# Eight PSUM banks in one rotation, and both halves of an expert's first layer open at once

## The chip, the core and the metric

One Trainium2 chip, one of its cores. The metric is the device time of one execution in microseconds, the median of several runs. The engines are TensorE (PE in the profile, with PEld for its weight loads), VectorE (DVE), ScalarE (ACT), GpSimd (POOL) and SyncE (SP), which issues most of the transfers.

## The reference

An mLSTM cell over 4 batches, 8 heads, 768 steps and 40 channels gives 3072 rows of 320 numbers. Each row then goes through one of 8 experts, chosen by a hash of its token, which is a two-layer network with 1024 hidden units:

```python
def _moe_ref(x, token_ids, w1, w2):          # x (3072, 320), w1 (8, 320, 1024), w2 (8, 1024, 320)
    expert_idx = token_ids * np.int64(2654435761) % np.int64(E)
    out = np.zeros((N, D), dtype=np.float32)
    for e in range(E):
        mask = expert_idx == e
        if not mask.any():
            continue
        xe = x[mask]
        h = np.maximum(xe @ w1[e], 0.0)
        out[mask] = h @ w2[e]
    return out.astype(np.float32)
```

Everything is fp32.

## The kernel before

The first 140 us or so compute the mLSTM cell in chunks of 128 steps, sort the tokens by expert and store the rows of the result in memory. The change does not touch that part. Its PSUM pool is closed before the experts begin.

**Experts.** The rows of an expert lie in 416 slots (CAP): three tiles of 128 and a remainder of 32. Expert 0 is computed plainly, half of its first layer already inside the mLSTM part. Experts 1 to 7 pass through the loop `for e in range(E)`, whose order of calls is the order in which each engine receives its instructions; no scheduler moves them (`tc.manual_schedule()`). For an expert e from 1 on that order is:

1. `fetch(e + 2)`: POOL gathers the rows of a later expert, SP stores them to memory and reads them back in blocks (`blocks`); `load_weights(e + 2)` on SP.
2. `differences_of_w2`: four POOL operations for the second layer (tile `tw`).
3. `layer1_by_seven`: the first layer.
4. POOL copies the remainder columns of h into `hrem`.
5. `layer2` for the third tile of 128 slots: eight matmuls of 320 columns (L1030), then ACT copies the result out and POOL scatters it.
6. `sums_of_w1` for the next expert, four DVE operations (tile `sw`).
7. After experts 3 and 7, `rest`: the second layer of four experts' remainders (L1143).
8. `layer2_by_seven`: the second layer for the other two tiles of slots, 4 x 7 matmuls of 160 columns (L1063). In its middle (`meanwhile`) DVE makes the differences of the next expert's rows (`sums_of_x`, tile `tx`).

**The first layer.** Of the 320 inputs the first 256 are two blocks of 128 rows, and the last 64 are a half block. The two full blocks, two blocks of hidden units and two halves of the slots make a 2 x 2 x 2 product, which is computed with seven block products in place of eight, in Winograd's form: sums of w1's blocks (`sw`) are multiplied with differences of the rows (`tx`). DVE and ACT put the products together with the intermediate tiles m, u and v. The 64 inputs are added by `halves` (L996): matmuls that use 64 of the array's 128 rows, issued in pairs, one on the lower and one on the upper rows, into two different banks.

The layer is done in two halves, g = 0 and g = 2, each with four blocks of hidden units. A half uses four PSUM banks and issues, on PE: products 0, 1, 2, 3 and 0 again (10 matmuls, L988), eight matmuls of 64 rows (L996), products 2 and 3 again (4 matmuls, L988). `product` issues two matmuls each time. After the first five products of the half g = 0 comes `meanwhile(g)`, which for experts 3 to 6 is a DVE transpose of the next expert's rows (`turned`, L1129). At the end of each half `done(g)` makes the sums of h for the second layer (`sums_of_h`, L942 to L945, tile `sh`): on POOL for g = 0, on DVE for g = 2.

**PSUM.** The pool `mps` has three kinds of tiles: `tp` for transposes and `zp` for second-layer results, two buffers each, and `mh` with four. Each of the first layer's halves takes all four `mh`, and so does `layer2_by_seven`. The second half of a layer therefore takes the banks of the first half.

**Buffers.** m1, u2 and u4 have one buffer each, `tx` has two. h (tile `h0`) is the same tile for all experts.

Of the kernel before, what the change touches and what calls it, by code (L numbers as in the profile page):

```python
# [8 lines left out]
F32 = mybir.dt.float32  # L9
# [8 lines left out]
P = 128  # L18
# [4 lines left out]
def kernel(  # L23
# [24 lines left out]
    nc = tc.nc  # L48
# [4 lines left out]
    Dm = H * D  # L53
    E, _, F = moe_w1.shape
    FB = F // P
# [8 lines left out]
    DB = len(dch)  # L64
# [49 lines left out]
    W = {}  # L114
# [790 lines left out]
    xp = ctx.enter_context(tc.tile_pool(name="xp", bufs=2))  # L905
    mps = ctx.enter_context(tc.tile_pool(name="mps", bufs=2, space=PSUM))

    def scatter(zp, idx, apart):
        zo = xp.tile([P, Dm], F32, name="zo", bufs=4)
        nc.scalar.copy(zo[:], zp[:])  # L910
        scatter_rows(zo, idx, apart)

    def scatter_rows(zo, idx, apart):
# [8 lines left out]

    def turn(xg, dst, on_act):

        tp = mps.tile([P, DB, P], F32, name="tp")
        for db in range(2):
            nc.tensor.transpose(tp[:, db, :], xg[:, db * P : (db + 1) * P], ident[:])
        nc.vector.tensor_copy(xg[:, Dm:], xg[:, 2 * P : Dm])
        nc.tensor.transpose(tp[:, 2, :], xg[:, 2 * P :], ident[:])
        if on_act:  # L930
            nc.scalar.copy(dst, tp[:])
        else:
            nc.vector.tensor_copy(dst, tp[:])

    def bank(i):
        return mps.tile([P, CAP], F32, name="mh", bufs=4)

    HC, HD = CAP // 2, Dm // 2

# [20 lines left out]

    def sums_of_x(xT):

        tx = xp.tile([P, 4, HC], F32, name="tx")
        b = [xT[:, i, j * HC : (j + 1) * HC] for i in range(2) for j in range(2)]
        differences(*b, [tx[:, i] for i in range(4)], nc.vector)
        return tx

    def layer1_by_seven(w, sw, xT, tx, h, meanwhile, done):

        w1t, w1c, _ = w  # L970
        lo, hi = slice(0, HC), slice(HC, CAP)

        def add(o, a, b):
            nc.vector.tensor_tensor(o, a, b, op=ALU.add)  # L974

        def pair(t):
            return t.rearrange("p (a c) -> p a c", a=2)

        for g in range(0, FB // 2, 2):
            bank = [mps.tile([P, CAP], F32, name="mh", bufs=4) for _ in range(4)]  # L980
            hv = h[:, 2 * g : 2 * g + 4].rearrange("p (a i) c -> p a i c", i=2)

            def block(fp, i, j):
                return w1t[:, j, (2 * fp + i) * P : (2 * fp + i + 1) * P]

            def product(n, lhsT, rhs, first=False):
                for a in range(2):
                    nc.tensor.matmul(  # L988
                        pair(bank[n])[:, a], lhsT=lhsT(g + a), rhs=rhs, start=first and a == 0, stop=True, skip_group_check=True,
                    )  # L990

            def halves(first, second):
                for a in range(2):
                    for i, (n, r) in enumerate((first, second)):
                        k = slice(i * P // 2, (i + 1) * P // 2)
                        nc.tensor.matmul(  # L996
                            pair(bank[n])[:, a], lhsT=w1c[k, g + a, :], rhs=xT[k, 2, r], start=False, stop=True, skip_group_check=True,
                        )

            m, u, v = [xp.tile([P, CAP], F32, name=n, bufs=1) for n in ("m1", "u2", "u4")]  # L1000
            product(0, lambda fp: block(fp, 0, 0), xT[:, 0, lo], True)
            nc.scalar.copy(m[:], bank[0][:])
            product(1, lambda fp: sw[:, 1, fp], tx[:, 1], True)
            add(u[:], m[:], bank[1][:])
            product(2, lambda fp: sw[:, 0, fp], tx[:, 0], True)
            add(v[:], m[:], bank[2][:])
            product(3, lambda fp: sw[:, 2, fp], tx[:, 2], True)
            add(v[:], v[:], bank[3][:])
            meanwhile(g)
            product(0, lambda fp: block(fp, 0, 1), xT[:, 1, lo])  # L1010
            halves((0, lo), (1, hi))
            nc.scalar.activation(hv[:, :, 0, lo], pair(bank[0]), AF.Relu)  # L1012
            add(hv[:, :, 1, hi], pair(v), pair(bank[1]))
            nc.scalar.activation(hv[:, :, 1, hi], hv[:, :, 1, hi], AF.Relu)
            halves((2, hi), (3, lo))
            product(2, lambda fp: sw[:, 3, fp], xT[:, 1, hi])
            add(hv[:, :, 0, hi], pair(u), pair(bank[2]))
            nc.scalar.activation(hv[:, :, 0, hi], hv[:, :, 0, hi], AF.Relu)
            product(3, lambda fp: block(fp, 1, 1), tx[:, 3])
            for a in range(2):  # L1020
                o = h[:, 2 * (g + a) + 1, lo]
                add(o, pair(u)[:, a], pair(bank[3])[:, a])
                nc.scalar.activation(o, o, AF.Relu)
            done(g)

    def layer2(w, h, js, idx, apart, between=lambda j: None, within=lambda j, fb: None):
        for j in js:
            zp = mps.tile([P, Dm], F32, name="zp")
            for fb in range(FB):
                nc.tensor.matmul(  # L1030
                    zp[:], lhsT=h[:, fb, j * P : (j + 1) * P], rhs=w[2][:, fb, :],
                    start=(fb == 0), stop=(fb == FB - 1),
                )
                within(j, fb)
            scatter(zp, idx(j), apart)
            between(j)
# [15 lines left out]
    def layer2_by_seven(w, tw, h, sh, idx, meanwhile):  # L1052

        w2t = w[2]
        bank = [mps.tile([P, CAP], F32, name="mh", bufs=4)[:, :HD] for _ in range(4)]
        m, u, v = [xp.tile([P, CAP], F32, name=n, bufs=1)[:, :HD] for n in ("m1", "u2", "u4")]
        zs = [xp.tile([P, Dm], F32, name="zo", bufs=4) for _ in range(2)]
        lo, hi = slice(0, HD), slice(HD, Dm)

        def products(*them):  # L1060
            for f in range(FB // 2):
                for n, lhsT, rhs, first in them:
                    nc.tensor.matmul(  # L1063
                        bank[n], lhsT=lhsT(f), rhs=rhs(f), start=first and f == 0, stop=f == FB // 2 - 1, skip_group_check=True,
                    )

        def rows(i, j):
            return lambda f: h[:, 2 * f + j, i * P : (i + 1) * P]

        def cols(j, r):  # L1070
            return lambda f: w2t[:, 2 * f + j, r]

        def of(t, i):
            return lambda f: t[:, i, f]

        def add(o, a, b):
            nc.vector.tensor_tensor(o, a, b, op=ALU.add)

        products((0, rows(0, 0), cols(0, lo), True), (1, of(sh, 1), of(tw, 1), True))
        nc.scalar.copy(m, bank[0])  # L1080
        add(u, m, bank[1])
        products((2, of(sh, 0), of(tw, 0), True), (3, of(sh, 2), of(tw, 2), True))
        add(v, u, bank[2])
        add(zs[1][:, hi], v, bank[3])
        meanwhile()
        products((0, rows(0, 1), cols(1, lo), False))
        nc.scalar.copy(zs[0][:, lo], bank[0])
        products((2, of(sh, 3), cols(1, hi), False), (3, rows(1, 1), of(tw, 3), False))
        add(zs[0][:, hi], u, bank[2])
        add(zs[1][:, lo], u, bank[3])  # L1090
        for j in range(2):
            scatter_rows(zs[j], idx(j), True)
# [4 lines left out]
    with tc.manual_schedule():  # L1097
# [39 lines left out]
            nc.gpsimd.tensor_copy(xT0[:, :, NM:], remT[:, :, :RM])  # L1137

        def rest(g):
            zp = mps.tile([P, Dm], F32, name="zp")  # L1140
            for fb in range(FB):
                for i in range(EG):
                    nc.tensor.matmul(  # L1143
                        zp[i * RM : (i + 1) * RM, :], lhsT=hrem[g][:, i, fb, :], rhs=W[g * EG + i][2][:, fb, :],
                        start=(fb == 0), stop=(fb == FB - 1),
                    )
            scatter(zp, cols_of(s_idx, NR + g)(0), True)
# [6 lines left out]
        for e in range(E):  # L1154
# [7 lines left out]
            if e == 0:  # L1162
                layer2(W[0], h, range(2), cols_of(s_idx, 0), True, lambda j: j == 0 and turn_third(), lambda j, fb: (j, fb) == (1, FB - 3) and turn_rest())
                layer1(W[0], xT0, h, 2 * P, CAP, bank)
                turned(1)
                tx = sums_of_x(xTs[1])
            else:
                tw = differences_of_w2(W[e])
                sh = xp.tile([P, 4, FB // 2, P], F32, name="sh", bufs=1)
                layer1_by_seven(  # L1170
                    W[e], sw, xTs[e], tx, h, lambda g: g == 0 and 2 < e < E - 1 and turned(e + 1),
                    lambda g: sums_of_h(h, sh, g, nc.vector if g else nc.gpsimd),
                )
            nc.gpsimd.tensor_copy(hrem[g][:, i], h[:, :, NM:])
# [65 lines left out]
```

## Time and profile before

| | us |
|---|---|
| median of three runs | 359.0 |
| the three runs | 355.92, 359.00, 360.87 |
| profiled execution, its own time | 359.64 |
| its span, first to last instruction | 357.6 |
| PE busy in the span | 339.2 (95%) |
| DVE busy | 226.9 (63%) |
| POOL busy | 214.3 (60%) |
| ACT busy | 138.5 (39%) |
| mean granted PE clock | 0.987 |

In the chain of work that ended last, PE has 76% of the span. By line the largest shares are L988 (first layer, 128 rows) with 20%, L1063 (second layer by seven) with 13%, L1030 with 8% and L996 (first layer, 64 rows) with 6%. The starts of experts 1 to 7 on PE are at 160.98, 187.47, 212.84, 242.85, 268.22, 293.59 and 318.96 us; PE's last matmuls end shortly before 349 us, and the rest of the span is the last scatter and the end of the program.

How to read the views: a row of the timeline has start, length, engine, line, operation, output and inputs, shape and count, and in brackets the idle time before it with what ended it. fp32 matmuls and their weight loads are shown as two records per instruction, so eight matmuls of L996 stand as x16. "issue" as a releaser means that nothing the profile shows was waited for.

### The profile page before, as it was taken

The numbers are of one execution on the slowest core, as the hardware profiler recorded it, in microseconds if no ns is written. First come the engines' busy times: TensorE is split into PE (matmuls) and PEld (weight loads), VectorE is DVE, ScalarE is ACT, GpSimd is POOL, SyncE is SP. The second block draws the span as 40 slices with busy tenths as digits, with TensorE's granted clock in tenths as the row PEclk, the third lists the DMA queues.
The fourth block names the chain that finished last, engine by engine and source line by source line (L and its number), as shares of the span: only waits on it lengthen the run. The fifth ranks groups of instructions, "written<-read, shape, count | busy, mean of one in ns | idle before, by whom it ended". The sixth has DMA issues, their size and how long they took to land.

```text
span 357.6 us, 9206 instructions
## 1 busy us (share of the span) xinstructions
PE 339.2 (95%) x3573; PEld 292.5 (82%) x3573; DVE 226.9 (63%) x512; ACT 138.5 (39%) x325; POOL 214.3 (60%) x301
## 2 busy tenths in 40 slices
PE   7899999999999699999999999999999999999990
PEld 6677898888888577788899899689899899898870
DVE  8867897998887551056665777726666757645310
ACT  6676688776675451113213212212313212213200
POOL 8822778899885546407717938816927829329221
PEclk9999999999999899999999999999999999999996
DMA  6699999989989964689878959495486592010010
GB/s 128 115 175 163 178 177 182 198 184 193 190 159 238 245 192 112 172 226 288 220 220 220 303 97 358 119 233 194 114 223 213 114 289 75 0 37 19 17 39 3
DMA packets 162358, 59.18 MB, mean 165 GB/s; under 512 B 140171, under 2 KB 158119, under 8 KB 162313
## 3 DMA queue, kind: packets, MB, share of 16 engines
q1 hardware_dynamic: 158377, 49.05, 58.8%
q0 software_dynamic: 2832, 9.34, 8.1%
q8 instruction: 29, 0.48, 0.6%
q10 hardware_dynamic: 1104, 0.18, 0.3%
q14 instruction: 16, 0.13, 0.1%
HBM read 46.48 MB, written 12.38 MB: 165 GB/s over the span
## 4 chain that ended last, share of the span: by engine, by line
PE 76%; DMA 6%; issue 5%; DVE 4%; SPq 4%; POOL 2%; ACT 1%; ACTq 0%; POOLq 0%; DVEq 0%
PE mh L988 20%; PE mh L1063 13%; PE zp L1030 8%; PE mh L996 6%; PE sp L447 6%; PE tr L390 5%; PE xh L505 5%; PE xh L499 3%; PE ab L405 3%; PE xh L478 2%; SPq L1125 2%; DMA w1t<-in_moe_w_dram 2%; SPq L237 1%; DMA R<-gate_rows 1%; PE zp L1143 1%
## 5 line engine op out<-in xcount | busy, mean ns | idle before, releaser
L914 POOL DMA_INDIRECT out_dram<-zo,s_idx x26 | 27.6, 1061 | 76.5 <-issue 46.7
L1030 PE MATMUL zp<-w2t,h 128*128 128x320 f32 x160 | 45.0, 433 | 0.5 <-ACT h L166 0.5
L974 DVE TENSOR_TENSOR h<-u,mh 128x416 f32<-128x416 f32 (+1 forms) x56 | 25.4, 475 | 25.0 <-PE mh L988 12.7
L1030 PEld LDWEIGHTS zp<-w2t,h 128*128 128x128 f32 x160 | 30.0, 190 | 11.8 <-ACT h L166 0.9
L505 PE MATMUL xh<-v,w 128*64 128x41 f32 x768 | 35.3, 224 | 0.0
L414 ACT ACTIVATE w<-ab 128x512 f32<-128x512 f32 x48 | 26.2, 596 | 19.0 <-PE ab L405 18.1
L453 DVE TENSOR_TENSOR w<-sp,w 128x512 f32<-128x512 f32 x48 | 30.8, 681 | 3.6 <-ACT w L414 3.6
L988 PE MATMUL mh<-tx,sw 128*128 128x208 f32 x168 | 31.9, 340 | 0.7 <-DVE sw L944 0.7
L505 PEld LDWEIGHTS xh<-v,w 128*64 128x64 f32 x768 | 31.5, 140 | 0.0
L988 PEld LDWEIGHTS mh<-tx,sw 128*128 128x128 f32 x168 | 29.7, 190 | 1.0 <-DVE sw L944 1.0
L110 POOL DMA_INDIRECT xg<-x_rows,g_idx x24 | 23.4, 975 | 9.0 <-issue 6.7
L447 PE MATMUL sp<-qT,kT 64*128 64x128 f32 x384 | 28.1, 285 | 0.3 <-ACT qT L395 0.3
L499 PE MATMUL xh<-C,qs 128*64 128x82 f32 x320 | 28.0, 253 | 0.0
L1063 PE MATMUL mh<-tw,sh 128*128 128x160 f32 x168 | 27.4, 299 | 0.0
L522 POOL TENSOR_TENSOR x<-x,og 128x320 f32<-128x320 f32 x24 | 20.6, 864 | 10.7 <-ACT og L439 8.6
L447 PEld LDWEIGHTS sp<-qT,kT 64*128 64x128 f32 x384 | 23.5, 187 | 4.2 <-issue 2.5
L974 DVE TENSOR_TENSOR u<-m,mh 128x416 f32<-128x416 f32 x28 | 16.5, 588 | 13.3 <-PE mh L988 6.8
L1012 ACT ACTIVATE h<-mh 128x416 f32<-128x416 f32 x14 | 7.2, 518 | 44.5 <-PE mh L996 44.5
L1063 PEld LDWEIGHTS mh<-tw,sh 128*128 128x128 f32 x168 | 24.3, 190 | 0.0
L988 PE MATMUL mh<-xT,w1t 128*128 128x208 f32 x112 | 24.3, 339 | 0.0
L996 PE MATMUL mh<-xT,w1c 64*128 64x208 f32 x224 | 23.5, 349 | 0.0
L488 POOL TENSOR_TENSOR C<-C,add 64x164 f32<-64x164 f32 x32 | 16.3, 510 | 9.8 <-ACT add L482 8.6
(241 smaller groups left out, 761.2 us busy)
## 6 DMA issues: line engine op xcount, KB each, us to landing
w2t<-in_moe_w_dram SPq DMA_DIRECT2D x7, 1280.0 KB
w1t<-in_moe_w_dram SPq DMA_DIRECT2D x7, 1024.0 KB
xb<-x_slots SPq DMA_DIRECT2D x84, 52.0 KB
k<-in_k_dram SPq DMA_DIRECT2D x24, 160.0 KB
v<-in_v_dram SPq DMA_DIRECT2D x24, 160.0 KB
og<-in_o_gate_dram SPq DMA_DIRECT2D x24, 160.0 KB
q<-in_q_dram SPq DMA_DIRECT2D x23, 160.0 KB
x_slots<-xg SPq DMA_DIRECT2D x7, 480.0 KB
```

Of the source, the lines that this page charges most:

```text
L110: nc.gpsimd.indirect_dma_start(out=xg, out_offset=None, in_=x_d[:rows, :], in_offset=bass.IndirectOffsetOnAxis(ap=idx, axis=0),)
L414: nc.scalar.activation(w[:, hf], ab[:], AF.Exp)
L447: nc.tensor.matmul(sp[hf][:, j, :], lhsT=d["kT"][r, j, :], rhs=d["qT"][r, j, :], start=True, stop=True)
L453: nc.vector.tensor_tensor(d["w"][:, hf], d["sp"][hf][:], d["w"][:, hf], op=ALU.mult)
L499: nc.tensor.matmul(xh[t, 2 * j : 2 * j + 2, :], lhsT=d["qs"][:, j, t], rhs=Cs[b][c % 2][:, j].rearrange("p h d -> p (h d)"), start=True, s ...
L505: nc.tensor.matmul(hs[t, 2 * j + hf, :], lhsT=d["w"][:, hf, j, t], rhs=d["v"][:, 2 * j + hf, :], start=(c == 0), stop=True, skip_group_che ...
L914: ins = nc.gpsimd.indirect_dma_start(out=out[:, :], out_offset=bass.IndirectOffsetOnAxis(ap=idx, axis=0), in_=zo[:], in_offset=None, bound ...
L974: nc.vector.tensor_tensor(o, a, b, op=ALU.add)
L988: nc.tensor.matmul(pair(bank[n])[:, a], lhsT=lhsT(g + a), rhs=rhs, start=first and a == 0, stop=True, skip_group_check=True,)
L996: nc.tensor.matmul(pair(bank[n])[:, a], lhsT=w1c[k, g + a, :], rhs=xT[k, 2, r], start=False, stop=True, skip_group_check=True,)
L1030: nc.tensor.matmul(zp[:], lhsT=h[:, fb, j * P : (j + 1) * P], rhs=w[2][:, fb, :], start=(fb == 0), stop=(fb == FB - 1),)
L1063: nc.tensor.matmul(bank[n], lhsT=lhsT(f), rhs=rhs(f), start=first and f == 0, stop=f == FB // 2 - 1, skip_group_check=True,)
```

## The change

All tiles of the experts come from one kind of PSUM tile, a full bank of 512 fp32, with eight buffers in one rotation (`psum`). `tp`, `zp` and `mh` become views of it.

`layer1_by_seven` becomes a generator per half, `half_layer`, with three stages, and the two halves advance stage by stage: first stage (ten matmuls) of g = 0, then of g = 2; `meanwhile` after both; second stage (the eight matmuls of 64 rows) of g = 0, then of g = 2; third stage (four matmuls and `done`) of g = 0, then of g = 2. Eight banks are open at once. u2 and u4 become one tile for each half (u20, u22, u40, u42), m1 stays one tile for both, and `tx` has one buffer in place of two. Within the second stage the four pairs of 64 rows of a half are issued together, ahead of the additions.

```diff
+    def psum():
+        return mps.tile([P, 4 * P], F32, name="mh", bufs=8)
...
-        tp = mps.tile([P, DB, P], F32, name="tp")
+        tp = psum().rearrange("p (d c) -> p d c", c=P)[:, :DB]
...
     def bank(i):
-        return mps.tile([P, CAP], F32, name="mh", bufs=4)
+        return psum()[:, :CAP]
...
-        tx = xp.tile([P, 4, HC], F32, name="tx")
+        tx = xp.tile([P, 4, HC], F32, name="tx", bufs=1)
...
-        for g in range(0, FB // 2, 2):
-            bank = [mps.tile([P, CAP], F32, name="mh", bufs=4) for _ in range(4)]
+        def half_layer(g):
+            bank = [psum()[:, :CAP] for _ in range(4)]
...
-            m, u, v = [xp.tile([P, CAP], F32, name=n, bufs=1) for n in ("m1", "u2", "u4")]
+            m, u, v = [xp.tile([P, CAP], F32, name=n, bufs=1) for n in ("m1", f"u2{g}", f"u4{g}")]
             product(0, lambda fp: block(fp, 0, 0), xT[:, 0, lo], True)
...
-            add(v[:], v[:], bank[3][:])
-            meanwhile(g)
+            add(v[:], v[:], bank[3])
             product(0, lambda fp: block(fp, 0, 1), xT[:, 1, lo])
+            yield
             halves((0, lo), (1, hi))
+            halves((2, hi), (3, lo))
             nc.scalar.activation(hv[:, :, 0, lo], pair(bank[0]), AF.Relu)
             add(hv[:, :, 1, hi], pair(v), pair(bank[1]))
             nc.scalar.activation(hv[:, :, 1, hi], hv[:, :, 1, hi], AF.Relu)
-            halves((2, hi), (3, lo))
+            yield
             product(2, lambda fp: sw[:, 3, fp], xT[:, 1, hi])
...
             done(g)
+            yield
+
+        parts = [half_layer(g) for g in range(0, FB // 2, 2)]
+        for stage in range(3):
+            for part in parts:
+                next(part)
+            if stage == 0:
+                meanwhile()
...
     def layer2(w, h, js, idx, apart, between=lambda j: None, within=lambda j, fb: None):
         for j in js:
-            zp = mps.tile([P, Dm], F32, name="zp")
+            zp = psum()[:, :Dm]
...
     def layer2_by_seven(w, tw, h, sh, idx, meanwhile):
...
-        bank = [mps.tile([P, CAP], F32, name="mh", bufs=4)[:, :HD] for _ in range(4)]
-        m, u, v = [xp.tile([P, CAP], F32, name=n, bufs=1)[:, :HD] for n in ("m1", "u2", "u4")]
+        bank = [psum()[:, :HD] for _ in range(4)]
+        m, u, v = [xp.tile([P, CAP], F32, name=n, bufs=1)[:, :HD] for n in ("m1", "u20", "u40")]
...
         def rest(g):
-            zp = mps.tile([P, Dm], F32, name="zp")
+            zp = psum()[:, :Dm]
...
                 layer1_by_seven(
-                    W[e], sw, xTs[e], tx, h, lambda g: g == 0 and 2 < e < E - 1 and turned(e + 1),
+                    W[e], sw, xTs[e], tx, h, lambda: 2 < e < E - 1 and turned(e + 1),
                     lambda g: sums_of_h(h, sh, g, nc.vector if g else nc.gpsimd),
                 )
```

More of the change, by code (lines that the diff above doesn't have):

```diff
@@ L906 @@
     mps = ctx.enter_context(tc.tile_pool(name="mps", bufs=2, space=PSUM))
+    def psum():
+        return mps.tile([P, 4 * P], F32, name="mh", bufs=8)
     def scatter(zp, idx, apart):
         zo = xp.tile([P, Dm], F32, name="zo", bufs=4)
-        nc.scalar.copy(zo[:], zp[:])
+        nc.scalar.copy(zo[:], zp)
         scatter_rows(zo, idx, apart)
@@ L977, in pair, with block @@
             return t.rearrange("p (a c) -> p a c", a=2)
-        for g in range(0, FB // 2, 2):
-            bank = [mps.tile([P, CAP], F32, name="mh", bufs=4) for _ in range(4)]
+        def block(fp, i, j):
+            return w1t[:, j, (2 * fp + i) * P : (2 * fp + i + 1) * P]
+        def half_layer(g):
+            bank = [psum()[:, :CAP] for _ in range(4)]
             hv = h[:, 2 * g : 2 * g + 4].rearrange("p (a i) c -> p a i c", i=2)
-            def block(fp, i, j):
-                return w1t[:, j, (2 * fp + i) * P : (2 * fp + i + 1) * P]
             def product(n, lhsT, rhs, first=False):
@@ L998, in halves @@
                         )
-            m, u, v = [xp.tile([P, CAP], F32, name=n, bufs=1) for n in ("m1", "u2", "u4")]
+            m, u, v = [xp.tile([P, CAP], F32, name=n, bufs=1) for n in ("m1", f"u2{g}", f"u4{g}")]
             product(0, lambda fp: block(fp, 0, 0), xT[:, 0, lo], True)
-            nc.scalar.copy(m[:], bank[0][:])
+            nc.scalar.copy(m[:], bank[0])
             product(1, lambda fp: sw[:, 1, fp], tx[:, 1], True)
-            add(u[:], m[:], bank[1][:])
+            add(u[:], m[:], bank[1])
             product(2, lambda fp: sw[:, 0, fp], tx[:, 0], True)
-            add(v[:], m[:], bank[2][:])
+            add(v[:], m[:], bank[2])
             product(3, lambda fp: sw[:, 2, fp], tx[:, 2], True)
-            add(v[:], v[:], bank[3][:])
-            meanwhile(g)
+            add(v[:], v[:], bank[3])
             product(0, lambda fp: block(fp, 0, 1), xT[:, 1, lo])
+            yield
             halves((0, lo), (1, hi))
+            halves((2, hi), (3, lo))
             nc.scalar.activation(hv[:, :, 0, lo], pair(bank[0]), AF.Relu)
@@ L1024, in layer1_by_seven @@
             done(g)
+            yield
[5 more added lines that the diff above has]
+                meanwhile()
     def layer2(w, h, js, idx, apart, between=lambda j: None, within=lambda j, fb: None):
         for j in js:
-            zp = mps.tile([P, Dm], F32, name="zp")
+            zp = psum()[:, :Dm]
             for fb in range(FB):
                 nc.tensor.matmul(
-                    zp[:], lhsT=h[:, fb, j * P : (j + 1) * P], rhs=w[2][:, fb, :],
+                    zp, lhsT=h[:, fb, j * P : (j + 1) * P], rhs=w[2][:, fb, :],
                     start=(fb == 0), stop=(fb == FB - 1),
```

## The prediction

> **What bounds the kernel now.** I read the table of busy stretches first, one row for each of experts 1 to 7. Those rows cover 160.7 to 345 us; of expert 0 before them the change touches only which bank a tile gets. From expert 2 on TensorE has no free time, as in this row:
>
> ```profile
> core 0: us, PE busy (x) PEld busy (x) DVE busy (x) ACT busy (x) POOL busy (x), PEclk, DMA share, GB/s
> ...
> 268.20:293.60 25.40, 25.40 (x163) 23.13 (x161) 16.78 (x33) 6.33 (x15) 15.93 (x15) 1.00 0.69 196
> ```
>
> Expert 5 takes 25.40 us and PE is busy for 25.40 of them at full clock; DVE has 8.6 us to spare and POOL 9.5. The list of what PE waited for gives two entries for all experts together, one at the start of expert 1 and one in expert 0:
>
> ```profile
> PE mh L988 <- DVE sw L944: 0.7, 1, 0.7
> ...
> PE zp L1030 <- ACT h L166: 0.5, 1, 0.5
> ```
>
> So no wait for a PSUM bank delays PE before the change, and a freer rotation has none to remove. What can shrink is PE's own time, so next I read the chain of waits through expert 5 (start, length, engine, line; two records stand for each matmul):
>
> ```profile
> 268.22 3.52 PE mh L988 x20
> 271.73 1.61 PE mh L996 x16
> 273.34 5.12 PE mh L988 x28
> 278.46 1.61 PE mh L996 x16
> 280.07 1.60 PE mh L988 x8
> 281.67 4.31 PE zp L1030 x16
> ```
>
> The reader is to divide. Twenty records in 3.52 us are 0.176 us each. A piece of 8 should then take 1.41 us and takes 1.60; one of 28 should take 4.93 and takes 5.12: each follows a run of L996 and is 0.19 too long. L996 is the matmul of 64 rows. Its records run in pairs, so 16 are 8 steps: 1.41 us, and they take 1.61, 0.20 too long. Entering and leaving one such run thus costs 0.39 us. PE's weight loads show the place:
>
> ```profile
> 271.66 1.36 PEld L996 LDWEIGHTS mh<-xT,w1c 64*128 64x128 f32 x16 [0.25 <-issue]
> 273.27 0.65 PEld L988 LDWEIGHTS mh<-xT,sw 128*128 128x128 f32 x4 [0.25 <-issue]
> ```
>
> Weight loads, which otherwise stand ahead of their matmul, stop for 0.25 us at both ends, waiting for nothing the trace can name. And the longest L996 matmul takes 440 ns against a median of 336, the longest of L988 that follows it 443 against 339: the first of a run is 104 ns longer.
>
> **What the Trainium skill says.** "TensorEngine Tiling (Array Packing)", section Tiling Modes: changing the tiling mode drains TensorE. The trace agrees in kind (64*128 against 128*128 rows, with the stops just shown); the page gives no price, so 0.39 us from the chain is used. "PSUM — Partial Sum Buffer", section Specifications: eight banks of 2 KiB per partition. Eight tiles of 512 fp32 are all of them; no row of the trace shows banks. "SBUF — State Buffer", section SBUF: two separate sides: a DVE operation with two SBUF inputs and a GpSimd operation hold one port pair in turn. The trace agrees in direction: POOL's sums of h take 0.92, 0.90 and 0.79 us in expert 2 beside DVE's, and 0.72, 0.73 and 0.73 in expert 6. I use it to price the slow rival.
>
> **Part 1: the runs.** Per expert 1 to 7 the order of PE becomes: first stage of both halves, one run of 16 matmuls of 64 rows, last stage of both. Matmuls and shapes stay; 14 runs become 7. Removed: 7 entries and 7 exits, 7 x 0.39 = 2.7 us, all on the path, since PE never idles there. The trace has no run of this length in the experts. Its bounds: nothing saved, if the excess grew with the run instead of being paid at its ends; and 0.41 us per run (2.9) if a record takes 0.1757 us, as the chain's piece of 14 records in 2.46 us says. I take 0.39, since the lengthened records stand at the ends.
>
> **Part 2: the order behind it.** Take expert 5 from its start T = 268.22. After the change the first stages end at T+7.04, the run at T+7.04+0.20+2.82 = T+10.06, the last matmul at T+10.06+0.19+2.82 = T+13.07 (before: T+13.45). Three users of h come closer:
>
> - The second layer's first eight matmuls (L1030). They need half 0's h at T+13.07 and half 1's 2.15 us later. Half 0's last stage ends at T+11.66. In the trace ACT's last ReLU ends 1.27 us after such a stage (276.05 against 274.78), so all of half 0 is ready at T+12.9, and the columns this product reads after about T+12. Half 1's are ready at about T+14.3, needed at T+15.2. Nothing is added.
> - POOL's sums of half 0 (four operations, L942 to L945). Before, half 0 was ready at T+7.8; now it is at T+12.9, and POOL, being in order, also holds the remainder copy and the next scatter behind them. But here POOL is late anyway:
>
> ```profile
> 279.88 1.54 POOL L952 TENSOR_TENSOR tw<-w2t,tw 128x640 f32<-128x640 f32 x1
> 281.38 0.73 POOL L942 TENSOR_TENSOR sh<-h 128x256 f32<-128x256 f32 x1
> 282.07 0.72 POOL L943 TENSOR_TENSOR sh<-h 128x256 f32<-128x256 f32 x1
> 282.87 0.79 POOL L944 TENSOR_TENSOR sh<-sh,h 128x256 f32<-128x256 f32 x1
> ```
>
>   They begin at T+13.2, behind the differences of w2, and the third, which PE needs first, ends at T+15.4. PE needs it 0.27 us into the seven products: T+13.07+4.31+0.27 = T+17.65. Slack 2.2 us. In experts 6 and 7 POOL has fewer gathers and starts at about T+9.3 now; there the sums move by 3.6 us to T+12.9 and end in the same slack. In expert 2 four gathers make POOL late: the third sum ends at 204.03+0.79 = 204.82 and PE comes at 205.23+0.27 = 205.50; 0.39 earlier still leaves 0.3 us. Cost 0; with no cover, at most the 0.39 of that one expert.
> - DVE's sums of half 1. They follow its last additions as before, 0.6 us after PE's last matmul, take 0.80+0.94+0.83 us, and are needed 0.54 us after POOL's. Cost 0.
>
> The 1.47 us transpose of the next tokens (L1129, experts 3 to 6) moves from T+3.35 to about T+7.0 on DVE. Queued behind it are half 0's and half 1's additions to h, 0.59 each: finished at about T+9.0 and T+9.8, before the last stage asks for DVE at T+10.95. Who waits for those is ACT, busy 6.3 of 25.4 us. The transpose's input is handed back 3.6 us later; the transfer that refills it follows a gather of the next expert. SP's and POOL's queues keep their order, and no DMA moves.
>
> **Part 3: banks and buffers.** Per expert 13 tiles, or 14 with a remainder, go round eight banks. The nearest reuse is half 1 taking the banks of the seven products just before: their last reader, DVE's two copies (267.98 for 0.59), ends at T+0.35, and they are written from T+3.52. The product buffers m1, u and v: only m1 stays single, and half 1's copy into it needs half 0's second addition, done by T+2.8, at T+4.2. The single buffer for differences of x is rewritten in the seven products, over 4 us after its last matmul. Cost 0 each. A freer rotation could also gain nothing, since PE waited for no bank; bounds 0 and 0. Expert 0's tiles come out of the rotation too: its first wait (0.5 us) is for h, its second for w1 of expert 1, both untouched.
>
> **Sum.** -2.7 us, and 0 to +0.39 for expert 2. The profiled execution took 359.64 us, 357.6 of span and 2.0 around it; 359.64-2.7 = 356.9. It stands 0.6 above the median of the three runs, 359.0; against that, 356.3, which I forecast: 0.8%.
>
> **Rivals.**
>
> - **The gain is not there (359.0, or 0 to 1 us under it).** The excess would grow with the run, or PE would stop at the seam between the halves because half 1's banks still await DVE. Against it: the lengthened records stand only first in a run, and the seam comes at T+8.6 while half 1's additions end at about T+7.0. 16%.
> - **POOL's sums of half 0 become the bound (slower).** The place is the second matmul of the seven products. It decides once the third sum ends after T+17.65. With the port taken in turn, each POOL operation could wait for a DVE sum of up to 0.97 us: 13.2+3x(0.75+0.97) = T+18.4, a stall of 0.7 in 7 experts, 4.9-2.7: 361.2. If DVE's four 0.69 us sums of the next w1 came in between as well, 2.8 us more at worst: 7x3.5-2.7 = 21.8, 381. For it: POOL's and DVE's sums do overlap. Against it: they overlap already, at 0.9 us and not 1.7. 9%, of which 6% above 2%.
> - **More than 2% faster.** It would take 7.2 us. All 14 runs' ends together are 14 x 0.39 = 5.5, and PE's waits 1.2. No view offers it: 2%, mostly for the scatter of the runs.
>
> **How the numbers follow.** The forecast has 73%. Two per cent, 7.2 us, is about what a measurement of this kernel can tell from no change: its three runs alone lie from 355.9 to 360.9. The chances are faster 0.03, within 0.91, slower 0.06. For the range: the gain lies between 0 and 2.9 us, and a median of three runs within about 2.5 of its centre; that gives 356.1-2.5 = 353.6 below, and 359.0+1.5 = 360.5 above, which takes in the first rival and leaves out most of the second.
>
> **What would show it.** The chain of an expert should have one piece of the 64-row matmuls, x32 in about 3.0 us, between pieces of the 128-row ones of 7.04 us ahead and 2.8+0.19 behind; experts 2, 4, 5 and 6 should take 25.0 us each and no longer 25.4; PE's weight loads should show seven pairs of 0.25 stops and not fourteen. PE still without waits for POOL or DVE. I am wrong if PE waits for sh at the seven products, if the run of 32 takes 3.2 us or more, or if PE shows idle time at the seam or for a bank.

## The result, and the profile after

| | before | after |
|---|---|---|
| median of 20 runs each, us | 359.0 | 355.5 |
| lowest and highest | 355.9, 362.0 | 353.8, 357.8 |
| span of the profiled execution | 357.6 | 355.2 |

The ratio is 0.992, with a 95% interval of 0.9897 to 0.9943. Against 359.0 that is a gain of 2.9 us, between 2.0 and 3.7: small, but more than nothing. The predicted gain was 2.7.

The row of the table of busy stretches for expert 5 after the change:

```profile
core 0: us, PE busy (x) PEld busy (x) DVE busy (x) ACT busy (x) POOL busy (x), PEclk, DMA share, GB/s
...
267.03:292.00 24.97, 24.97 (x161) 23.20 (x161) 17.02 (x33) 6.42 (x15) 15.72 (x15) 1.00 0.68 188
```

PE is still busy for the whole of its expert at full clock; the expert is 24.97 us long. Before, the chain put expert 5 between 268.22 and the start of the next at 293.59, 25.37: 0.40 less. Experts 1, 4, 6 and 7 gain the same, expert 2 gains 0.36 and expert 3 0.32 (30.01 before, 29.69 after): 2.7 in all. Where it went is in the chain of waits of the changed kernel (start, length, engine, line, records; L991 are the 128-row products, L999 the 64-row matmuls, L1042 the third tile, L1075 the seven products):

```profile
267.03 7.03 PE mh L991 x40
274.06 3.01 PE mh L999 x32
277.08 3.01 PE mh L991 x16
280.09 4.31 PE mh L1042 x16
284.39 7.61 PE mh L1075 x56
292.00 7.03 PE mh L991 x40
```

Divide as in the prediction. Forty records in 7.03 us are 0.1757 each. The 32 records of L999 are 16 steps, 2.81 us, and take 3.01. The 16 behind them should take 2.81 and take 3.01. A run still costs 0.20 at each end, exactly as it did when it was half as long, and an expert now has one run in place of two. The weight loads have one stop on the way in and one on the way out per expert:

```profile
273.99 2.76 PEld L999 LDWEIGHTS mh<-xT,w1c 64*128 64x128 f32 x32 [0.25 <-issue]
277.00 0.65 PEld L991 LDWEIGHTS mh<-xT,sw 128*128 128x128 f32 x4 [0.25 <-issue]
```

The list of what the weight loads waited for counts them, seven each way, where each stood at 14 (3.5 us) before:

```profile
PEld mh L999 <- issue: 1.8, 7, 0.3
PEld mh L991 <- issue: 1.8, 7, 0.3
```

Across experts 1 to 7 the list of what PE waited for is empty. The 0.7 us for the sums of w1 at the start of expert 1 are gone too, but that is no gain of the change: in this execution expert 1 began 1.25 us later (162.23 against 160.98), since PE waited longer in the part ahead of the experts, where nothing was changed:

```profile
PE ab L405 <- DMA R<-gate_rows: 3.6, 1, 3.6
PE tr L390 <- DMA q<-in_q_dram: 1.4, 2, 0.9
```

Before, these were 2.8 and 0.6 us. Such a list shows idle time only, and a wait costs a little more: matmuls that follow one another are shown overlapping by 0.16 us, and the first one after a wait is 0.1 us longer. So the 0.7 cost 0.95 us. The spans add up: 357.6 - 2.7 (runs) - 0.95 (the wait that the later start swallowed) + 1.25 (the longer head) = 355.2, as measured.

The sums on POOL that the prediction watched, in expert 5:

```profile
278.71 1.56 POOL L955 TENSOR_TENSOR tw<-w2t,tw 128x640 f32<-128x640 f32 x1
280.22 0.75 POOL L945 TENSOR_TENSOR sh<-h 128x256 f32<-128x256 f32 x1
280.91 0.92 POOL L946 TENSOR_TENSOR sh<-h 128x256 f32<-128x256 f32 x1
281.91 0.79 POOL L947 TENSOR_TENSOR sh<-sh,h 128x256 f32<-128x256 f32 x1
```

The third ends at 282.70. It is the weights (`sh`) of the second of the seven products, so PE needs it when it loads them:

```profile
284.37 0.33 PEld L1075 LDWEIGHTS mh<-tw,sh 128*128 128x128 f32 x2
```

A slack of 1.67 us. In expert 2 there is none. The same lines there (the third sum, the weights of the first and second product, and from the chain all seven products):

```profile
203.93 0.79 POOL L947 TENSOR_TENSOR sh<-sh,h 128x256 f32<-128x256 f32 x1
...
204.29 0.46 PEld L1075 LDWEIGHTS mh<-w2t,h 128*128 128x128 f32 x2
204.77 0.30 PEld L1075 LDWEIGHTS mh<-tw,sh 128*128 128x128 f32 x2
...
204.73 7.64 PE mh L1075 x56
```

The sum ends at 204.72 and the load starts 0.05 us later, 0.48 behind the load ahead of it where expert 5 has 0.41. The seven products take 7.64 us and not 7.61: too little for the list of waits, but the cover is used up.

### The profile page after: what moved, and what is told of

It is laid out like the page before. It is cut to its first block, busy times and chain, and to the rows that moved or that the text cites. A ratio compares the mean times of both kernels' runs of the same rounds, so it can differ in the third digit from the quotient of the medians.

```text
span 355.2 us, 9214 instructions
## 1 busy us (share of the span) xinstructions
PE 336.3 (95%) x3573; PEld 293.8 (83%) x3573; DVE 229.8 (65%) x512; ACT 139.4 (39%) x325; POOL 215.1 (61%) x301
## 4 chain that ended last, share of the span: by engine, by line
PE 84%; DMA 4%; issue 4%; DVE 3%; ACT 2%; SPq 1%; POOL 1%; POOLq 0%
PE mh L991 20%; PE mh L1075 13%; PE mh L1042 12%; PE sp L447 6%; PE mh L999 6%; PE tr L390 6%; PE xh L505 5%; PE mh L157 3%; PE ab L405 3%; PE xh L499 3%; PE xh L478 2%; DMA k<-in_k_dram 2%; DMA R<-gate_rows 1%; PE mh L1155 1%; PE xb L418 1%
## 5 line engine op out<-in xcount | busy, mean ns | idle before, releaser
L917 POOL DMA_INDIRECT out_dram<-zo,s_idx x26 | 26.8, 1030 | 69.5 <-issue 47.2
L1042 PE MATMUL mh<-w2t,h 128*128 128x320 f32 x160 | 45.0, 433 | 0.5 <-ACT h L166 0.5
L1042 PEld LDWEIGHTS mh<-w2t,h 128*128 128x128 f32 x160 | 30.0, 190 | 11.8 <-ACT h L166 0.9
L991 PE MATMUL mh<-tx,sw 128*128 128x208 f32 x168 | 31.8, 339 | 0.0
L991 PEld LDWEIGHTS mh<-tx,sw 128*128 128x128 f32 x168 | 29.7, 190 | 0.0
L1075 PE MATMUL mh<-tw,sh 128*128 128x160 f32 x168 | 27.4, 299 | 0.0
L1075 PEld LDWEIGHTS mh<-tw,sh 128*128 128x128 f32 x168 | 24.3, 190 | 0.0
L991 PE MATMUL mh<-xT,w1t 128*128 128x208 f32 x112 | 23.1, 339 | 0.0
L913 ACT COPY zo<-mh 128x320 f32<-128x320 f32 x12 | 5.1, 426 | 42.6 <-PE mh L1042 27.3
L422 DVE TENSOR_TENSOR qs<-qT,xb 128x512 f32<-128x512 f32 x20 | 13.7, 683 | 12.6 <-PE xb L418 12.6
```

Of the source, the lines that this page charges most:

```text
L917: ins = nc.gpsimd.indirect_dma_start(out=out[:, :], out_offset=bass.IndirectOffsetOnAxis(ap=idx, axis=0), in_=zo[:], in_offset=None, bound ...
L991: nc.tensor.matmul(pair(bank[n])[:, a], lhsT=lhsT(g + a), rhs=rhs, start=first and a == 0, stop=True, skip_group_check=True,)
L1042: nc.tensor.matmul(zp, lhsT=h[:, fb, j * P : (j + 1) * P], rhs=w[2][:, fb, :], start=(fb == 0), stop=(fb == FB - 1),)
L1075: nc.tensor.matmul(bank[n], lhsT=lhsT(f), rhs=rhs(f), start=first and f == 0, stop=f == FB // 2 - 1, skip_group_check=True,)
```

## The experiments

Theory: **the ends**. Each run of 64-row matmuls costs 0.4 us, whatever its length, and nothing else in the change moves the time. Rivals: the **rotation** (eight banks open) is what pays; the excess grows with the **number of 64-row matmuls**; and, for what limits a further gain, **POOL's sums**. The ratios are to the kernel before, timed on the same chip. Unless said otherwise the edits are to the changed kernel.

### The rotation without joined runs, two ways

In the first, both halves' first stages stay open together, and then each half finishes by itself, so there are 14 runs as before. In the second the halves follow each other whole, as before; only the banks rotate.

```diff
-        for stage in range(3):
-            for part in parts:
-                next(part)
-            if stage == 0:
-                meanwhile()
+        for part in parts:            # first way
+            next(part)
+        meanwhile()
+        for part in parts:
+            next(part)
+            next(part)
...
+        for n, part in enumerate(parts):   # second way
+            next(part)
+            if n == 0:
+                meanwhile()
+            next(part)
+            next(part)
```

> The changed kernel with its 64-row run cut in two again: both first stages open together, then second and third stage of g = 0, then of g = 2. 14 runs for experts 1 to 7 in place of 7. If a run costs 0.39 to 0.40 us at its ends (my theory): 2.8 us slower than the changed kernel, so level with the kernel before, ratio 1.000, an expert 25.37 us. If the open halves and banks bring the gain and not the runs: ratio 0.992, an expert 24.97 us.

> The changed kernel's eight banks in one rotation and its separate u and v, but the halves computed wholly one after the other as before. My theory: the rotation is worth nothing, ratio 1.000 to the kernel before, PE without waits for a bank, an expert 25.37 us. If the rotation frees PE of waits that the records hide: ratio 0.996 or less.

Measured: first way 357.9 against 357.7, ratio 0.9992 (0.9964 to 1.0020); second way 357.6 against 357.7, 1.0001 (0.9977 to 1.0026). The chain of the first way through expert 5:

```profile
267.24 7.03 PE mh L991 x40
274.27 1.61 PE mh L999 x16
275.88 1.60 PE mh L991 x8
277.48 1.61 PE mh L999 x16
279.09 1.60 PE mh L991 x8
```

The same matmuls with the first stages joined, but two runs: 1.61 and 1.60 are back twice, and the expert takes 25.37 us, as in the second way. So eight open banks, the separate u and v and the joined first stages are worth nothing by themselves, within 0.4%. They only make room for the joined run.

### More runs: four and eight an expert

From the first way above, product 2 is put between a half's two groups of 64-row matmuls (28 runs in all), and then every two 64-row matmuls stand apart (56). No matmul is added or taken away. The lines up to the second mark of a gap are the 28 runs; the rest are the 56, where `halves` and `product` are told which of their two steps to issue.

```diff
             halves((0, lo), (1, hi))
-            halves((2, hi), (3, lo))
...
             product(2, lambda fp: sw[:, 3, fp], xT[:, 1, hi])
+            halves((2, hi), (3, lo))
...
+            halves((0, lo), (1, hi), (0,))                               # 56 runs: third argument: which a
+            product(2, lambda fp: sw[:, 3, fp], xT[:, 1, hi], these=(0,))
+            halves((0, lo), (1, hi), (1,))
...
+            product(2, lambda fp: sw[:, 3, fp], xT[:, 1, hi], these=(1,))
+            halves((2, hi), (3, lo), (0,))
+            product(3, lambda fp: block(fp, 1, 1), tx[:, 3], these=(0,))
+            halves((2, hi), (3, lo), (1,))
```

> As the two-run kernel, with product 2 of a half put between its first and its last four 64-row matmuls: 28 runs. Same matmuls. Price at the ends: 14 x 0.40 = 5.6 us over the kernel before, about 364.6, ratio 1.016, an expert 26.2 us. Price per matmul of 64 rows: ratio 0.992 to 1.000, no dependence on the number of runs.

> Each two 64-row matmuls apart, with one full matmul between: 56 runs. Price at the ends: 42 x 0.40 = 16.8 us over the kernel before, about 375.8, ratio 1.047, an expert 27.8 us. If a short run costs less than a long one, for example half, about 367 and ratio 1.023. Price per matmul: 1.000.

| runs in an expert | in seven experts | expert 5, us | ratio to before (95%) |
|---|---|---|---|
| 1 (the change) | 7 | 24.97 | 0.992 (0.990 to 0.994) |
| 2 | 14 | 25.37 | 0.999 (0.996 to 1.002) |
| 4 | 28 | 26.17 | 1.015 (1.010 to 1.021) |
| 8 | 56 | 27.76 | 1.047 (1.042 to 1.053) |

The chain with eight runs, where one piece of each kind is enough:

```profile
281.70 0.55 PE mh L999 x4
282.26 0.55 PE mh L991 x2
```

Two steps are 0.35 us and take 0.55, on the 64-row side and on the 128-row side. The expert grows by 0.40 for one more run, 1.20 for three, 2.79 for seven: 0.40 each, on a straight line through runs of 32, 16, 8 and 4 records. That excludes the rival in which the excess grows with the number of 64-row matmuls, which is the same in all rows. "TensorEngine Tiling (Array Packing)" of the Trainium skill, section Tiling Modes, says that a change of tiling mode drains TensorE. The runs agree that the change itself is what costs, and give it a size here: 0.20 us per change for matmuls of 208 fp32 columns. What the array does in that time no trace shows. The part of the kernel ahead of the experts mixes such forms too; no other order was tried there.

### How far away POOL's sums are

The changed kernel, with two and then five extra copies of POOL's first sum ahead of the real ones in each expert.

```diff
         a = [v[:, :, j, i * P : (i + 1) * P] for i in range(2) for j in range(2)]
+        if eng is nc.gpsimd:
+            for _ in range(2):                                           # or 5
+                eng.tensor_tensor(sh[:, 2, g : g + 2], a[0], a[2], op=ALU.subtract)
```

> The changed kernel with two more POOL operations (the first sum of h, done twice more) ahead of POOL's sums of half 0, in each of experts 1 to 7: 1.5 to 1.8 us later. In the changed kernel's trace the third sum ends 2.0 us before PE needs it in experts 4 and 5, 3.0 in 1, 6 and 7, 6.2 in 3, but 0.3 in expert 2. My theory: PE stalls in expert 2 alone, 1.2 to 1.6 us, ratio to the kernel before 0.996. If POOL's sums are already the bound and the slack is not there: 1.5 us in each of seven experts, about 11 us, ratio 1.02.

> The same with five more operations, 3.8 to 4.6 us later. From the same slacks: about 1.2 us of stall in experts 1, 6 and 7, 3.9 in 2, 2.2 in 4 and 5, none in 3: 12 us over the changed kernel (9 to 15), about 367, ratio 1.025. This is the slow rival of the prediction made true; it should appear in PE's waits as sh for the seven products.

With two: 359.3 against 360.8, ratio 0.9974 (0.9950 to 0.9999), half a per cent behind the changed kernel's 0.992. PE has two waits, one of them not expected (start, length, engine, line, operation, tiles; in brackets the idle time before it and what ended it):

```profile
205.06 0.54 PE L1078 MATMUL mh<-tw,sh 128*128 128x160 f32 x2 [1.76 <-POOL sh L947]
232.30 4.49 PE L1158 MATMUL mh<-w2t,hrem 128*32 128x320 f32 x58 [1.60 <-POOL hrem L1189]
```

The first is expert 2, which had no slack left: counted from the first of the seven products, the third sum ends 1.98 us later than in the changed kernel (205.00 against 202.86, and 204.72 against 204.56), and PE loses all of it, 1.76 us idle and 0.26 at the stall itself. In experts 4 and 5 the extra work just uses up the slack of about 1.7 us: PE's load of the sums starts 0.05 us after the third sum there too (261.99 and 287.02), and the seven products take 7.63 and 7.66 us. The others, with 2.67 us and more, swallow it. The second is the copy of the remainder, which stands behind the sums on POOL and is needed by `rest` in expert 3. The prediction had named that copy as held behind the sums, but priced only the sums.

With five: 386.8 against 360.8, ratio 1.073 (1.065 to 1.080). The expectation of about 12 us was far too low; the span grew by 30.7. The list of waits:

```profile
PE mh L1078 <- POOL sh L947: 16.5, 6, 5.1
PE mh L1158 <- POOL hrem L1189: 4.5, 1, 4.5
```

That is 21.0 us: every expert now stalls. Counted from expert 1's second product to the last `rest`, the experts take 32.5 us longer; this execution entered them 1.5 us earlier. The five extra operations took 0.79 us each in the mean, and the three real sums behind them 0.94, 1.10 and 1.01 where 0.75, 0.92 and 0.79 stood above. The rest lies in PE itself. The same seven products in expert 1 of this kernel, twice in the table of busy stretches:

```profile
core 0: us, PE busy (x) PEld busy (x) DVE busy (x) ACT busy (x) POOL busy (x), PEclk, DMA share, GB/s
180.50:183.90 3.40, 3.36 (x15) 3.36 (x16) 1.64 (x2) 0.29 (x1) 2.88 (x3) 0.63 0.47 161
183.90:187.50 3.60, 3.60 (x25) 3.60 (x25) 1.39 (x4) 0.00 (x0) 0.00 (x0) 0.87 0.74 144
```

Following a stall of 1.94 us the granted clock falls, and the products behind the stall take 9.28 us where those of expert 7, after a stall as long, take 7.60: 1.68 more. This happened after four of the six stalls for sums, three times with this loss and once with 1.4, and `rest` after its 4.53 us took 7.18 in place of 4.49: 3 x 1.68 + 1.4 + 2.7 = 9.1. With 0.26 for each of the seven stalls, 21.0 + 9.1 + 1.8 = 31.9 of the 32.5. So the slow rival is real, and expert 2 stands at its edge; but what made it costly here was extra POOL work, not the change.

### Without the 64-row matmuls

The matmuls of the last 64 inputs of experts 1 to 7 are left out, to measure what the run is worth as a whole.

```diff
             yield
-            halves((0, lo), (1, hi))
-            halves((2, hi), (3, lo))
```

> The changed kernel without the 64-row matmuls of experts 1 to 7: it leaves out the last 64 of the 320 inputs of their first layer. PE's path is 8 x 2 x 0.176 + 0.39 = 3.2 us shorter in each, 22.5 in all. If PE alone set the end: ratio 0.93. My theory: POOL's sums come out as the next bound, late by 2.9 us in expert 2, 1.2 in 4 and 5, 0.3 in 1, so about 17 us under the changed kernel, ratio 0.945.

Measured: 349.6 against 360.8, ratio 0.972 (0.963 to 0.981); a miss. Seven runs of 3.01 + 0.20 us are 22.5 us of PE, but the span fell by 8.9 only, and the experts by 7.8, since this execution entered them 1.1 us earlier. The list of waits has what took their place:

```profile
PE mh L1040 <- ACT h L1020: 5.0, 5, 1.4
PE mh L1073 <- POOL sh L947: 2.6, 4, 1.5
PE mh L1153 <- POOL hrem L1184: 2.3, 1, 2.3
```

Stalls of 9.9 us in ten places, 0.26 more at each, and the half clock again after the 2.3 us one (0.54 granted for the next 3.7 us, so about 1.7 lost). 22.5 - 9.9 - 2.6 - 1.7 = 8.3, where 7.8 was measured. The largest entry was not foreseen. The second layer's first product (L1040 here) waits for ACT's ReLU of the upper columns of half 0. In the changed kernel the same two are close in expert 5, though nothing waits:

```profile
278.64 0.55 ACT L1022 ACTIVATE h<-h 128x416 f32<-128x416 f32 x1 [1.02 <-DVE h L977]
...
279.75 4.13 PEld L1042 LDWEIGHTS mh<-w2t,h 128*128 128x128 f32 x16
```

The ReLU is done at 279.19, and PE loads these columns as weights 0.56 us later: the run of 64-row matmuls is itself time in which DVE and ACT work on h. Taking it out saved about a third of its length.

### Expert 0's runs, and the wait behind them

Expert 0's second part of the first layer still has two runs. One function more, `layer1_in_one_run`, puts them together: the 128-row matmuls of the first four blocks of hidden units, then all eight matmuls of 64 rows, then the 128-row matmuls of the other four, with eight banks open.

```diff
-                layer1(W[0], xT0, h, 2 * P, CAP, bank)
+                layer1_in_one_run(W[0], xT0, h, 2 * P, CAP, bank)
```

> The changed kernel with the lesson carried to expert 0: the second part of its first layer opens all eight banks and has one run of 16 matmuls of 64 rows in place of two of 8. One run less, 0.3 to 0.4 us of PE's time. If nothing else sets the pace there: ratio to the kernel before 0.991 in place of 0.992, too little to be told by the times, so the trace has to show it. The rival: the sums of w1 for expert 1 wait for the transfer of w1, which lands at a time of its own, and PE waits at the first products that use them by as much as it has gained; then the start of expert 1's second product does not move and the ratio is 0.992.

Measured: 355.4 against 358.0, ratio 0.9933 (0.9884 to 0.9981), the same as the change. The run was joined: from the last transpose within expert 0 PE reaches expert 1 in 11.4 us in place of 11.8. The gain was given back one piece later:

```profile
PE mh L1024 <- DVE sw L980: 1.0, 1, 1.0
```

PE waits for the sums of expert 1's w1, whose first operation waited in turn for the transfer of w1. Most of these executions have such a wait (0.68 us before the change, 0.40 and 0.88 with 14 runs); the changed kernel's has none, as its expert 1 began late.

```profile
160.84 0.69 DVE L978 TENSOR_TENSOR sw<-w1t 128x512 f32<-128x512 f32 x1 [0.56 <-DMA w1t<-in_moe_w_dram]
```

So w1 was issued earlier, ahead of the store and the block reads of expert 1's rows, w2 behind them; once with the kernel as changed, and once with expert 0's run joined as well.

```diff
         fetch(0)
+        load_weights(1, later=True)      # w1 alone
         fetch(1)
         blocks(1)
-        load_weights(1)
+        nc.sync.dma_start(W[1][2][:], moe_w2[1].rearrange("(a p) d -> p a d", p=P))
```

> The changed kernel with the transfers of w1 for expert 1 put ahead of that expert's block reads on SP's queue, where they were behind them; w2 stays behind. If w1's landing is what DVE's sums, and so PE, wait for at the head of expert 1 (0 to 0.9 us in the runs so far): the wait goes or shrinks to 0.2, and the kernel is 0.3 to 0.7 us faster than the changed one, ratio to the kernel before 0.990 to 0.991. If the block reads then land later by as much as w1 lands earlier: DVE's transpose is late in its place and nothing is gained, ratio 0.992.

> The same and expert 0's single run of 64 rows. Now the run's 0.3 to 0.4 us should not be given back to a wait: 0.8 to 1.1 us under the changed kernel, ratio 0.989 to 0.990, and in the trace PE should enter expert 1's second product without a wait or with one under 0.3 us. If the wait comes back at 1 us, from the transpose: 0.992.

Measured: 360.5 against 362.3, 0.9958 (0.9932 to 0.9984), and with the joined run 361.0 against 362.3, 0.9968 (0.9940 to 0.9996). Both ratios lie above the change's 0.992, though their intervals overlap with its own; the gain hoped for did not come. The issues on SP in the changed kernel, and with w1 early:

```profile
145.49 0.38 SPq L1122 DMA_DIRECT2D x_slots<-xg  x1
149.02 6.13 SPq L1137 DMA_DIRECT2D xb<-x_slots  x12
```

```profile
146.02 0.38 SPq L1123 DMA_DIRECT2D x_slots<-xg  x1
153.03 6.02 SPq L1138 DMA_DIRECT2D xb<-x_slots  x12
160.72 1.48 DVE L1142 STREAM_TRANSPOSE xT<-xb 128x1248 f32<-128x1248 f32 x1 [4.05 <-DMA xb<-x_slots]
165.58 3.95 PE L992 MATMUL mh<-tx,sw 128*128 128x208 f32 x12 [2.35 <-DVE sw L948]
```

The block reads follow the store of the rows. With w1's transfers beside it, they were issued 7.0 us after the store and not 3.5 (8.7 with the joined run); that those transfers held the store up fits, but no run separates it. So the transpose of expert 1's rows waited 4 us, and with it everything queued behind it on DVE: the sums of w1 stand there too. w1 was in place early, and its sums came later than before. PE waited 1.10 us for the transposed rows and then 2.35 for the sums, and the clock fell again (0.53 for 3.5 us).

No version that computes the whole result came out below the changed kernel's ratio.

## Why the prediction was right

- **What bounds the kernel.** Right: the time of experts 1 to 7 follows PE's own work. The rotation by itself gave 1.000 and 0.999.
- **Part 1, the runs.** Right in mechanism and size. The run of 32 records takes 3.01 us (expected about 3.0) and the piece behind it 3.01. A run costs 0.40, the term in the sum was 0.39. Seven would be 2.8; experts 2 and 3 lost 0.1 of it, 0.03 of that to POOL's sums and the rest mostly in `rest` (4.52 us for 4.45). That the experts' gain is just the 2.7 forecast is in that much luck. What had only been read from the lengthened first records was shown by the line through 7, 14, 28 and 56 runs.
- **Part 2, the order behind it.** Right that next to nothing was added. Half 0's h was ready at T+12.75 (expected T+12.9), half 1's at T+14.16 (T+14.3), the transpose began at T+6.87 (T+7.0). The slack of POOL's sums was misread in the prediction: it was counted to the second product's own turn on PE, but the sums are loaded as its weights before that. Counted as the prediction did, expert 5 has 1.96 us in place of 2.2; to the load it is 1.67. In experts 6 and 7 it is 2.67 to the load, more than foreseen. In expert 2, where 0.3 us should have been left, nothing was: before the change the third sum ended at 204.82, and its load was only 0.38 us behind it,

```profile
205.20 0.33 PEld L1063 LDWEIGHTS mh<-tw,sh 128*128 128x128 f32 x2
```

  and the two runs' 0.40 us took all of that. PE lost 0.03 us, inside the bound of 0.39 that the prediction set for this expert; that it was so little is luck. In expert 5 the third sum also ended 0.2 us later than forecast (T+15.7), as POOL's second took 0.92 us in place of 0.72; DVE's sums now begin 0.5 us after POOL's and not 0.9. That agrees in direction with the shared port that the prediction used, but the operation grew by less than any of the DVE operations beside it takes (0.55 to 0.89 us). The closest cover but expert 2's is that of the second layer's first product: the columns that it reads were ready 0.56 us ahead of their load (by the text's figures about 1, to the product itself), and with the run taken out this became the largest wait.
- **Part 3, banks and buffers.** Right: no wait for a bank, at the seam or elsewhere.
- **The sum.** 356.3 forecast, 355.5 measured. The ratio puts the gain at 2.9, the chain at 2.7; the rest of the 3.5 us between the medians lies within the spread of the runs.
- **The rivals.** That the gain would not be there falls with the chain. That POOL becomes the bound did not happen, though expert 2 came to its edge; its place was right, and the copy of the remainder behind it was not priced. Had it happened, its price would have been set too low, since a stall of some 2 us can also cost 1.7 us of clock. That more than 2% could not come from these runs holds: joining expert 0's too gave nothing that could be measured.

## What to carry to other kernels

Divide the pieces of the bounding engine's chain by their records: an engine that is 100% busy can still hold time that belongs to changes between two forms of its own instructions, and the way to take it out is to collect one form in one run, which needs buffers to keep more results open. Such a saving is worth its count times its price only while the next engine's work stays covered, so work out the slack of each user of the result (where the result is loaded as weights, up to the load and not the matmul), of what stands behind it in the same queue, and of the slowest stage among those that look alike. Before an early transfer is issued earlier still, look at what it will run beside and at what stands ahead of its consumer in that consumer's queue.

## What was not expected of the hardware

**Short stalls that halve PE's clock.** "TensorE: Matmul & The Clock Gate" of the Trainium skill, section Why this matters for your kernels, warns of idle gaps of more than about 3 us. Here shorter ones did it: in the kernels with extra POOL work, without the 64-row matmuls and with w1 early, the clock fell after stalls of 1.94, 2.29, 3.14, 3.17, 4.53 and 5.14 us, and not after 1.17, 1.45, 1.52, 1.60, 1.76 and one of 1.95. It also fell after two of 2.35, but these came 1 us of work behind another stall, of 1.10 and of 2.57 us; after the 2.57 the four records between still ran at full speed. The seven products in expert 1 and expert 7 of the kernel with five extra sums, after almost the same stall:

```profile
180.54 0.54 PE L1078 MATMUL mh<-tw,sh 128*128 128x160 f32 x2 [1.94 <-POOL sh L947]
...
183.13 3.43 PE L1078 MATMUL mh<-tw,sh 128*128 128x160 f32 x18
...
338.90 0.54 PE L1078 MATMUL mh<-tw,sh 128*128 128x160 f32 x2 [1.95 <-POOL sh L947]
...
340.63 2.61 PE L1078 MATMUL mh<-tw,sh 128*128 128x160 f32 x18
```

The 18 records that are together in both took 3.43 us in the first and 2.61 in the second. A loss of 1.68 us agrees with half the clock for about 3.4 us, which is the length of the window that the page gives (section What's actually happening) as free-running; that the place of the stall within such a window decides would fit both cases, but no run here shows it.
